# The first batch's spectrum goes straight to its transform rows in SBUF, and the second batch's first sums read their first product from PSUM

## The chip, the cores and the metric

The kernel runs on one core of one Trainium2 chip. The metric is the time of one execution on the device in microseconds (us). The kernel before has a median of 1088.05 us over three runs (1087.7 to 1088.87).

## The reference

There are 8 batches of 4224 positions with 192 channels, in 8 heads of 24. First comes a causal convolution whose 7 taps differ at every position and head and are normalized by a softmax. Its result `x` gets the real part of its two-dimensional Fourier transform added; rows are then normalized and go through an MLP of 192, 768 and 192 channels with a residual.

```python
w = np.exp(weight_gen - np.max(weight_gen, axis=-1, keepdims=True))
w = w / (np.sum(w, axis=-1, keepdims=True) + 1e-09)
out = np.einsum('bshk,bskhg->bshg', w, x_unf)      # x_unf: 7 earlier rows of each position
...
X = np.fft.fft(np.fft.fft(x, axis=1), axis=2)
u = x + np.real(X)
un = (u - mu) / np.sqrt(var + 1e-06)
ch = np.maximum(un @ w_ch1, 0.0) @ w_ch2
return u + ch
```

All tensors are f32; the MLP weights arrive as f64 words, which the kernel turns into f32 itself.

## The kernel before, in words

**Layout.** The 4224 positions are 128 partitions of 33 rows. A batch is worked on in 9 chunks: chunk 8 is row 0, and each of the chunks 0 to 7 is four rows, two from the front (2c+1, 2c+2) and the two mirrored ones from the back, since the transform of a real signal wants both together.

**Convolution, `conv(b)`.** For each chunk and each tap, a product of the shifted rows in `x_sb` and the tap `wp`, spread over 24 channels, is made by VectorE (L762). `x_sb` lies in SBUF, `wp` in PSUM. How the seven products are added depends on the batch. In batch 0 the chunks of `PE_SUMS` (0, 1, 3, 5 and 7) are summed by TensorE, with f32 matmuls by the identity into two PSUM banks `pa` (L767, 128x384 each), which ScalarE copies to `u` (L779). The others are summed by POOL (L771, `u<-u,pr`). A few products of batch 0 are made by ScalarE in pieces of 24 channels (`ACT_TAPS`, L723) or by POOL (`POOL_TAPS`, L760). In batch 1 the chunks 0 and 1 have all their products on POOL; in the chunks 2 to 7 VectorE makes the seven products, the first into `u` itself, does the first of the six adds (`DVE_ADDS`, also L771), and POOL does the other five. From batch 2 on a wide form works on two chunks at once (L847 products on VectorE, L851 adds on POOL).

**Fold and spectrum.** POOL folds a chunk's mirrored rows into `sm` (L794, L795). TensorE multiplies `sm` by a cosine and sine table into `pg` (L803, PSUM tag "fft"). ScalarE keeps a half in `up`, and VectorE forms `gt` from both (L810, L813). Two DMAs for each pair of chunks write `gt` to a DRAM tensor `g_d` (L816, L817).

**Transform, mix and normalization.** `transform(b)` loads `g_d` in blocks of four triples of frequencies with 102 rows (L889, L891), multiplies them by tables (`pp`, L899, tag "fft") and ScalarE copies the result into `pq`. Each of the nine groups of four rows is then mixed: a matmul by the tables (`eo`, L930, tag "fft"), an evacuation on ScalarE to `ot`, and four adds on VectorE into `u` (L936 to L939). Means and variances come from VectorE for the first three groups (L960, L961, `QUICK`), which are also transposed on TensorE with matmuls by the identity (`tr`, L986); the others use ScalarE's sums and a transposing DMA. The steps L974 make the bias of each normalized row, and ScalarE writes `un` (L976).

**MLP.** First layer `ph` (L1060, L1027), rectified to `hh` (L1079, L1080), second layer `po` (L1094), residual on VectorE (L1099), and one output DMA for each half group. The weights' words are turned into f32 by seven VectorE instructions for each piece of 384 columns (L472 to L483) and split into f16 pairs (L488, L489); this is done while batch 0 waits for its transform.

**Filler.** `WARM` puts matmuls of the identity by itself (L538) into TensorE's queue: 14 at the start (`warm_x`) and 40 after the last chunk of batch 0 (`warm`).

**What sets the order.** All instructions are recorded first; `plan()` then lays out each engine's queue with a list scheduler that goes by `cost`, a table of estimated durations. Engines run their queues in order, so an instruction whose data are late holds up everything behind it on that engine. PSUM has eight banks, handed out by tags: "fft" two, "ph" three, "po" two and "wp" one. A tile of a tag can be written only when the tile that had its bank before has been read.

## Time and profile before

| | before |
|---|---|
| median of 3 runs | 1088.05 us |
| span of the profiled execution | 1087.9 us |
| TensorE busy | 1065.5 us (98%) |
| VectorE busy | 958.7 us (88%) |
| POOL busy | 857.1 us (79%) |
| ScalarE busy | 800.0 us (74%) |
| first MLP matmul starts | 100.68 us |

The profile is one execution, whose span is 0.15 us under the median of the runs. PE is TensorE, DVE VectorE, ACT ScalarE, POOL GpSimd and SP SyncE, whose queue issues the DMAs. A row of the groups gives line, engine, operation, output and inputs by the program's names, the shape, the count, busy time and mean ns of one, and behind the second bar the engine's idle time ahead of them with what ended it. Rows of a timeline or of the chain of waits begin with start and length in us. `L` numbers are lines of the kernel before; in the order rows below those of "now" are lines of the changed kernel.

### The profile page before, as it was taken

How to read it: one execution, taken by the hardware profiler on the slowest of the kernel's cores; microseconds unless marked ns; L12 is line 12 of the kernel's file. 1: busy time of each engine (PE TensorE's matmuls, PEld its weight loads, DVE VectorE, ACT ScalarE, POOL GpSimd, SP SyncE). 2: the span in 40 equal slices, each digit the busy share in tenths (PEclk: the TensorE clock that was granted, in tenths of full speed). 3: DMA queues.
4: the chain of work that ended last, by engine and by line, in shares of the span. 5: the costliest groups of instructions: out<-in, count | busy, mean ns of one | idle time of the engine just before them, and what ended most of it. 6: DMA issues, size and time to landing. Idle time of an engine off the chain costs nothing.

```text
span 1087.9 us, 23453 instructions
## 1 busy us (share of the span) xinstructions
PE 1065.5 (98%) x8600; PEld 802.9 (74%) x8600; DVE 958.7 (88%) x1639; ACT 800.0 (74%) x2414; POOL 857.1 (79%) x615
## 2 busy tenths in 40 slices
PE   7899999999999999999999999999999999999998
PEld 5477777787767877777778876887778777786767
DVE  8999999899989999899999999899999998355543
ACT  4666864679966878788786877678786878588842
POOL 5989699899969999799969999699969999011200
PEclk9999999999999999999999999999999999999999
DMA  9353135714492348623582348624582333623311
GB/s 323 129 146 115 34 94 141 202 46 111 119 259 80 85 115 206 170 67 85 129 248 79 92 109 220 157 57 121 122 205 68 83 68 89 140 56 76 79 53 48
DMA packets 171091, 131.20 MB, mean 121 GB/s; under 512 B 119067, under 2 KB 151776, under 8 KB 170976
## 3 DMA queue, kind: packets, MB, share of 16 engines
q1 hardware_dynamic: 170976, 129.70, 45.2%
q8 instruction: 68, 1.11, 0.4%
q14 instruction: 47, 0.39, 0.1%
HBM read 61.46 MB, written 39.37 MB: 93 GB/s over the span
## 4 chain that ended last, share of the span: by engine, by line
PE 66%; DVE 14%; POOL 5%; DMA 4%; ACT 3%; issue 3%; SPq 0%; DVEq 0%; ACTq 0%; POOLq 0%
PE po L1094 27%; PE ph L1060 24%; PE pp L899 5%; PE eo L930 4%; PE ph L1027 3%; DVE pr L847 3%; POOL u L771 2%; PE pg L803 2%; DVE hh L1080 2%; ACT pr L723 1%; DMA ht<-hl 1%; DVE pr L762 1%; POOL u L851 1%; DMA g<-g_d 1%; DMA ring<-ht 1%
## 5 line engine op out<-in xcount | busy, mean ns | idle before, releaser
L851 POOL TENSOR_TENSOR u<-u,pr 128x1536 f32<-128x1536 f32 x144 | 497.0, 3452 | 5.5 <-DVE pr L847 1.7
L1094 PE MATMUL po<-w2h,hh 128*128 128x192 f16 x2832 | 409.2, 247 | 0.0
L1094 PEld LDWEIGHTS <-hh 128*128 128x128 f16 x4248 | 359.1, 98 | 60.1 <-issue 15.2
L1060 PE MATMUL ph<-ht,w1h 128*128 128x512 f16 (+1 forms) x1296 | 382.7, 362 | 0.3 <-ACT ht L987 0.3
L1094 PE MATMUL po<-w2l,hh 128*128 128x192 f16 x1416 | 348.8, 246 | 0.0
L1080 DVE SCALAR_TENSOR_TENSOR hh<-ph,hh 128x512 f16<-128x512 f32 (+1 forms) x390 | 240.5, 636 | 60.9 <-ACT hh L1079 60.5
L1079 ACT ACTIVATE hh<-ph 128x512 f16<-128x512 f32 (+1 forms) x390 | 206.0, 550 | 89.2 <-PE ph L1060 41.0
L847 DVE TENSOR_TENSOR pr<-x_sb,wp 128x1536 f32<-128x1536 f32 x144 | 249.7, 1747 | 7.3 <-POOL u L851 7.3
L1060 PEld LDWEIGHTS <-w1h 128*128 128x128 f16 x1296 | 125.3, 98 | 97.9 <-issue 9.4
L1060 PE MATMUL ph<-ht,w1l 128*128 128x512 f16 (+1 forms) x528 | 181.7, 350 | 0.0
L996 ACT ACTIVATE un<-u,rs 128x192 f32<-128x192 f32 x252 | 122.2, 539 | 40.2 <-POOL rs L994 34.5
L1001 POOL TENSOR_TENSOR hl<-un,hl 128x512 f16<-128x512 f32 (+1 forms) x69 | 74.9, 1086 | 84.3 <-issue 42.5
L771 POOL TENSOR_TENSOR u<-u,pr 128x768 f32<-128x768 f32 (+1 forms) x72 | 117.9, 1649 | 12.2 <-DVE pr L762 11.4
L967 ACT ACTIVATE junk<-u,st 128x192 f16<-128x192 f32 x252 | 114.3, 453 | 4.4
L965 ACT ACTIVATE junk<-u 128x192 f16<-128x192 f32 x252 | 90.8, 360 | 27.6 <-DVE u L939 21.8
L1099 DVE SCALAR_TENSOR_TENSOR u<-po,isc,u 128x384 f32<-128x384 f32 (+1 forms) x122 | 73.1, 599 | 21.1 <-PE po L1094 20.7
L930 PEld LDWEIGHTS eo<-cs_sb,pq 97*128 97x128 f32 x544 | 78.3, 191 | 13.4 <-issue 4.4
L930 PE MATMUL eo<-cs_sb,pq 97*128 97x97 f32 x544 | 85.7, 275 | 0.0
L762 DVE TENSOR_TENSOR pr<-x_sb,wp 128x768 f32<-128x768 f32 (+1 forms) x91 | 74.7, 868 | 2.1 <-POOL u L771 0.7
L1060 PEld LDWEIGHTS <-w1l 128*128 128x128 f16 x528 | 51.9, 98 | 21.6 <-issue 0.5
L794 POOL TENSOR_TENSOR sm<-u 128x382 f32<-128x382 f32 x64 | 64.6, 1009 | 3.7 <-ACT u L779 3.2
L994 POOL TENSOR_TENSOR rs<-st,rs 128x4 f32<-128x4 f32 (+1 forms) x69 | 13.6, 201 | 67.4 <-DVE rs L970 67.3
(130 smaller groups left out, 1538.4 us busy)
## 6 DMA issues: line engine op xcount, KB each, us to landing
out_dram<-u SPq DMA_DIRECT2D x64, 384.0 KB
x_sb<-in_x_dram SPq DMA_DIRECT2D x48, 384.0 KB
g<-g_d SPq DMA_DIRECT2D x40, 336.0 KB
x_sb<-in_x_dram SPq DMA_DIRECT2D x8, 864.0 KB
g_d<-gt SPq DMA_DIRECT2D x32, 195.0 KB
g_d<-gt SPq DMA_DIRECT2D x32, 189.0 KB
w<-in_weight_gen_dram SPq DMA_DIRECT2D x6, 924.0 KB
x_sb<-in_x_dram SPq DMA_DIRECT2D x8, 672.0 KB
```

The lines of the kernel that those rows point to most:

```text
L762: last_product[b] = nc.vector.tensor_tensor(out=dst, in0=rows, in1=wk, op=ALU.mult)
L771: adder.tensor_tensor(out=u, in0=u, in1=pr, op=ALU.add)
L847: last_product[b] = nc.vector.tensor_tensor(out=pr.rearrange("p (s r) (h g) -> p s (r h) g", s=2, g=G), in0=rows, in1=wp[:, :, :, k:k + 1] ...
L851: nc.gpsimd.tensor_tensor(out=u, in0=u, in1=pr, op=ALU.add)
L930: last_mix[b] = nc.tensor.matmul(eo[:, e, j, :], lhsT=pq[0:DH, e, r, r:r + P], rhs=cs_sb[:, e, :], start=True, stop=True)
L965: nc.scalar.activation(junk, uv[t], AF.Identity, scale=-1.0 / D, accum_out=st[:, t, 0:1])
L967: nc.scalar.activation(junk, uv[t], AF.Square, bias=st[:, t, 0:1], accum_out=st[:, t, 1:2])
L996: nc.scalar.activation(un[:, t, :], uv[t], AF.Identity, bias=rs[:, 1, t:t + 1], scale=rs[:, 0, t:t + 1])
L1060: last_ph[n] = nc.tensor.matmul(ph[:, 0:T], lhsT=wt[:, cs_], rhs=ht[:, 0:T, blk], start=(i == 0 and not opens), stop=(i == len(terms) - 1 ...
L1079: nc.scalar.activation(a[:, 0:T], ph[:, 0:T], AF.Relu)
L1080: nc.vector.scalar_tensor_tensor(out=l[:, 0:T], in0=ph[:, 0:T], scalar=0.0, in1=a[:, 0:T], op0=ALU.max, op1=ALU.subtract)
L1094: nc.tensor.matmul(po[t // 2][:, t % 2, :], lhsT=hx[:, t], rhs=wx[:, c2, :], start=(c2 == 0 and i == 0), stop=(c2 == NH - 1 and i == len(t ...
```

## The change

1. **Batch 0's spectrum.** The table of the first transform is sorted so that frequencies 1 to 63 come as 21 triples (`NM`) and 0 and 64 as a block of their own. In batch 0, `gt` goes by DMA from SBUF to `g0`, a view of the space that batch 1's `u` will use later, in 17 large pieces and 18 small ones. Nothing of it is written to DRAM, and `transform(0)` reads `g0` without a load. Later batches still go through DRAM, with one write of 126 rows and one of 2 for each pair of chunks; the zeroing of `g_d` is gone.
2. **First products of batch 0.** In the chunks that TensorE sums, VectorE writes the first product straight into the two banks `pa`; ahead of it three f16 matmuls of the identity open each bank (`open_bank`).
3. **First sums of batch 1 (`ADD_PSUM`).** In the chunks 2 to 7 the first product goes into two PSUM banks `pf` of the tag "fft", 384 columns each, and VectorE's first add reads it there, also in two halves. Folds and spectra of a chunk are put into the next chunk.
4. **Opening.** The groups of chunks are (5,), (6, 7) at the end instead of (5, 6), (7,); chunk 7's product on ScalarE goes back to VectorE; the folds of chunks 5 and 7 run on VectorE. 18 warm matmuls follow chunk 6 in place of 40 after chunk 7. The first three groups are transposed by TensorE's transpose in place of a matmul by the identity.
5. **The planner's costs.** An add on VectorE with both inputs in SBUF is put at 2.0 ns a column instead of 1.042, POOL's products at 1.78, a transpose at one pass, and a DMA from SBUF to SBUF has an issue cost that grows with its rows. This moves instructions throughout the program.

Other edits have no instruction of their own behind them: constants for options that are off (`ONE_BIAS`, `SEEDED`, `PE_WORDS`, `POOL_OWN`, `POOL_WORDS`), `u` in fixed halves by a batch's parity instead of a rotation, and the planner's handling of partition strides. There is one scale more for the MLP (`fsc`).

The diff's core:

```diff
-ACT_TAPS = {(0, 1): (0,), (0, 3): (0,), (0, 5): (0,1), (0, 7): (0,)}
+ACT_TAPS = {(0, 1): (0,), (0, 3): (0,), (0, 5): (0,1)}
-WARM = {-1: 14, 7: 40}
+WARM = {-1: 14, 6: 18}
+DVE_FOLDS = (5, 7)
+OPENING = [(8, 0), (1, 2), (3, 4), (5,), (6, 7)]
...
+    def open_bank(bank):
+        for i in range(0, 2 * D, P):
+            nc.tensor.matmul(bank[:, i:i + P], lhsT=ident16, rhs=ident16, start=(i == 0), stop=False)
...
+                    seeds = pa if i == 0 and mine else None
+                    if ADD_PSUM and i == 0 and DVE_ADDS.get((b, c)):
+                        seeds = firsts[c] = [pst("fft", 2, [P, 512], F32, f"pf_{b}_{c}_{h}") for h in range(2)]
+                    elif seeds:
+                        for bank in seeds:
+                            open_bank(bank)
...
+                        if seeds:
+                            for h in range(2):
+                                last_product[b] = nc.vector.tensor_tensor(
+                                    out=seeds[h][:, 0:2 * D].rearrange("p (n g) -> p n g", g=G), in0=rows[:, h], in1=wk[:, h], op=ALU.mult)
...
+                        if i == 1 and c in firsts:
+                            for h, bank in enumerate(firsts.pop(c)):
+                                nc.vector.tensor_tensor(out=u[:, h], in0=bank[:, 0:2 * D].rearrange("p (r d) -> p r d", r=2), in1=pr[:, h], op=ALU.add)
+                            continue
...
+        if b == 0:
+            for j in range(J):
+                last_g2[0] = nc.sync.dma_start(g0[t2 + j:t2 + j + 6 * NT:NT, 0:NM], gt[0:6 * NM, at + j])
+            for kk in range(2):
+                last_g2[0] = nc.sync.dma_start(g0[kk * NT + t2:kk * NT + t2 + J, NM], gt[6 * NM + kk:6 * NM + kk + 1, at:at + J])
+        elif at == 2 or c == NC:
...
-            nc.sync.dma_start(g_d[0:NK1, 0, ts, :], gt[0:NK1, 0:at + J])
-            nc.sync.dma_start(g_d[1:NK1 - 1, 1, ts, :], gt[NK1:P, 0:at + J])
+            nc.sync.dma_start(g_d[0:NM, :, ts, :].rearrange("m k t d -> k m t d"), gt[0:6 * NM, 0:at + J])
+            nc.sync.dma_start(g_d[NM, 0:2, ts, :], gt[6 * NM:P, 0:at + J])
...
+            if b == 0:
+                g2 = g0[:, m0:m0 + nm]
...
-                    nc.tensor.matmul(tr[i][0:m, t, :], lhsT=un[:, t, i * P:i * P + m], rhs=ident32, start=True, stop=True)
+                    nc.tensor.transpose(tr[i][0:m, t, :], un[:, t, i * P:i * P + m], ident32)
...
+        t = 150 + (6.27 if ins.opcode == "Reciprocal" else 2.0 if slow else 1.042) * n + (60 if len(reads) == 3 and n < 512 else 0)
```

**What moves, first place.** VectorE's queue around the mix of group 0 of batch 0. The names `raw_w`, `pa_w`, `t_w`, `pw_w` and `w2f` are the turning of weight words into f32, `eo` and `ot` are the mix, `u` the rows. Before:

```order
L483 TENSOR_TENSOR w2f<-pw_w_0_1005,t_w_0_1006 128x384
L476 SCALAR_TENSOR_TENSOR pw_w_1_1015<-pa_w_1_1014,t_w_1_1016 128x384
L478 TENSOR_SCALAR pa_w_1_1014<-pw_w_1_1015 128x384
L481 SCALAR_TENSOR_TENSOR t_w_1_1016<-raw_w_416,pa_w_1_1014 128x384
L483 TENSOR_TENSOR w2f<-pw_w_1_1015,t_w_1_1016 128x384
L936 TENSOR_TENSOR eo_0_928<-eo_0_928,ot_0_933 128x2x97
L937 TENSOR_TENSOR eo_0_928<-eo_0_928,ot_0_933 128x194
L938 TENSOR_TENSOR u_0_145<-u_0_145,eo_0_928 128x2x2x97
```

Now, from the last weight steps ahead of the mix on:

```order
L495 TENSOR_SCALAR pa_w_0_977<-raw_w_433 128x384
L517 SCALAR_TENSOR_TENSOR w1l_90<-pw_w_00_878,sc_w_852,w1h_89 128x384
L497 SCALAR_TENSOR_TENSOR t_w_0_979<-raw_w_433,pa_w_0_977 128x384
L1001 TENSOR_TENSOR eo_0_901<-eo_0_901,ot_0_906 128x2x97
L517 SCALAR_TENSOR_TENSOR w1l_90<-pw_w_01_890,sc_w_852,w1h_89 128x384
L1002 TENSOR_TENSOR eo_0_901<-eo_0_901,ot_0_906 128x194
L498 TENSOR_SCALAR pa_w_0_977<-raw_w_433 128x384
L1003 TENSOR_TENSOR u_72<-u_72,eo_0_901 128x2x2x97
L1004 TENSOR_TENSOR u_72<-u_72,eo_0_901 128x2x2x95
L499 SCALAR_TENSOR_TENSOR pw_w_0_978<-pa_w_0_977,t_w_0_979 128x384
```

The first add of `eo_0` stood behind all weight steps and now stands ahead of twelve steps of the second layer's words. Seven of the twelve come before the steps that make group 0's bias (L1043 now), and five behind them.

**Second place.** VectorE's queue in a chunk of batch 1's convolution: `pr` is a product, `pf` a PSUM bank with half the first product. Before, chunk 3:

```order
L762 TENSOR_TENSOR u_2_1368<-x_sb,wp_815 128x768
L762 TENSOR_TENSOR pr_3_1_1464<-x_sb,wp_815 128x768 x2
L771 TENSOR_TENSOR u_2_1368<-u_2_1368,pr_3_1_1464 128x768
L936 TENSOR_TENSOR eo_5_1358<-eo_5_1358,ot_5_1400 128x2x97
L762 TENSOR_TENSOR pr_3_3_1506<-x_sb,wp_815 128x768
```

Now, the same chunk:

```order
L813 TENSOR_TENSOR pf_3_0_1422<-x_sb,wp_789 128x384
L813 TENSOR_TENSOR pf_3_1_1423<-x_sb,wp_789 128x384
L825 TENSOR_TENSOR pr_3_1_1433<-x_sb,wp_789 128x768 x2
L835 TENSOR_TENSOR u_73<-pf_3_0_1422,pr_3_1_1433 128x384
L835 TENSOR_TENSOR u_73<-pf_3_1_1423,pr_3_1_1433 128x384
```

The product of 768 into `u` became two of 384 into PSUM, and the add of 768 two of 384. The two `pr` products stand between them, as before.

**Third place.** SyncE's queue at the end of batch 0's spectrum, now: the pieces of the last two pairs of chunks (`gt_4`, `gt_6`) into `g0`, which is named after the space that it borrows (`u_73`). Before, four writes to DRAM and seven loads stood here.

```order
L876 DMA u_73<-gt_4_474 6x21x192 x4
L878 DMA u_73<-gt_4_474 2x1x192
L876 DMA u_73<-gt_6_659 6x21x192 x4
L878 DMA u_73<-gt_4_474 2x1x192 x3
L878 DMA u_73<-gt_6_659 2x1x192 x4
```

The last pair's rows leave in four large and four small pieces, with three small ones of the pair before among them.

More of the change, by code (lines that the diff above doesn't have):

```diff
@@ L199, in plan @@
                 needs.setdefault(index[first.name], False)
-        price = cost(ins, lane, reads, writes)
+        price = cost(ins, lane, reads, writes, sbuf)
         if joined:
@@ L652, in conv @@
                 keep_warm(pst("fft", 2, [P, P], F32, "warm_x"), WARM[-1])
-        groups = [(NC, 0), (1, 2), (3, 4), (5, 6), (7,)] if b == 0 else [(c,) for c in range(NC + 1)]
+        groups = OPENING if b == 0 else [(c,) for c in range(NC + 1)]
         if b >= WIDE_FROM:
@@ L726, in conv @@
                 for c, R, u, wp, pa, wq, pt, at in chunks:
-                    order = turns(pt, TURNS[len(pt)]) if pt and pa else range(K)
+                    order = turns(pt, TURNS[len(pt)]) if pa and 0 < len(pt) < K else range(K)
                     order = [k for k in order if k not in at] + list(at)
+                    mine = [k for k in range(K) if k not in pt and k not in at]
+                    if pa and mine:
+                        order.sort(key=lambda k: k != mine[0])
                     k = order[i]
```

245 lines of the change are left out of this document (144 added, 101 removed).

## The prediction

> **What bounds the kernel now.** I began with the page: span, busy shares and the chain that ended last.
>
> ```profile
> span 1087.9 us, 23453 instructions
> PE 1065.5 (98%) x8600; PEld 802.9 (74%) x8600; DVE 958.7 (88%) x1639; ACT 800.0 (74%) x2414; POOL 857.1 (79%) x615
> PE 66%; DVE 14%; POOL 5%; DMA 4%; ACT 3%; issue 3%; SPq 0%; DVEq 0%; ACTq 0%; POOLq 0%
> ```
>
> TensorE is busy for 1065.5 of 1087.9 us, so a gain must come from work that TensorE no longer has, from its 22.4 us of idle time, or from "busy" time that is only filler: the warm matmuls. The change touches batches 0 and 1, so I cut the span where the MLP begins and where the second batch is behind, with the view of busy time by window (span, then busy time of PE, PEld, DVE, ACT and POOL with counts, granted clock, DMA share, GB/s).
>
> ```profile
> 60.00:80.00 20.00, 19.75 (x125) 16.08 (x124) 18.43 (x44) 11.08 (x41) 16.16 (x15) 1.00 0.50 150
> 100.40:203.70 103.30, 98.52 (x553) 74.89 (x553) 100.51 (x175) 71.97 (x188) 91.99 (x75) 1.00 0.35 97
> 120.00:200.00 80.00, 75.50 (x425) 59.76 (x424) 78.48 (x133) 52.84 (x146) 75.84 (x62) 1.00 0.41 117
> 203.70:1088.00 884.30, 877.50 (x7603) 665.48 (x7601) 765.06 (x1274) 670.77 (x2001) 681.79 (x469) 1.00 0.45 115
> ```
>
> From 203.70 TensorE idles 6.8 us in 884.3. That stretch is its own; the change leaves its matmuls alone, so I carry its length over. Between 100.40 and 203.70, where batch 1 is convolved while batch 0 runs its MLP, TensorE idles 4.78 us and VectorE only 2.79. Before 100.40 nothing of the MLP has begun, and a microsecond won there moves everything behind it. Two numbers are therefore wanted: when the first MLP matmul starts, and how long the next hundred microseconds take. The chain of waits says what sets each.
>
> ```profile
> 61.15 5.34 ACT pr L723 x26
> 67.67 0.76 DVE wp L580
> 71.91 0.48 DVE pa_w L472
> ...
> 91.55 0.56 DVE w2f L483
> 92.42 0.38 DVE eo L937
> ...
> 96.58 0.56 ACT un L976
> 97.18 2.85 PE tr L986 x14
> 100.04 0.59 ACT ht L987
> 100.68 1.24 PE ph L1060 x5
> ```
>
> From 71.91 to 92.11 the chain holds VectorE work alone: words of the MLP weights turned into floats. The spectrum's way through DRAM, beside it, is not in the chain.
>
> ```profile
> by line: POOL u L771 23.0%; issue 13.0%; DVE pr L762 10.8%; PE ph L1060 10.2%; PE po L1094 6.0%; PE tr L986 3.8%; DVE u L762 2.7%; POOL hl L1001 2.7%; POOL hl L1003 2.3%; PE pp L899 2.3%; DVE wp L573 1.8%; DVE w L574 1.8%; POOL sm L794 1.7%
> ```
>
> This is the same chain grouped by line from 100 to 215 us: the convolution's adds on POOL and its products on VectorE, in turn.
>
> **Term 1, the opening.** The DMA hop first. Rows of SyncE's queue and of TensorE:
>
> ```profile
> 71.45 0.30 SPq L816 DMA_DIRECT2D g_d<-gt  x1
> 75.43 10.54 SPq L889 DMA_DIRECT2D g<-g_d  x6
> 72.31 7.41 PE L538 MATMUL warm<-ident 128*128 128x128 f32 x64
> 79.56 0.87 PE L899 MATMUL pp<-te_sb,g 102*97 102x102 f32 x8
> 89.95 2.21 PE L930 MATMUL eo<-cs_sb,pq 97*128 97x97 f32 x16
> ```
>
> From the last write's issue (71.45) to the first transform matmul (79.56) pass 8.1 us: 4.0 for the write up to the load's issue, 4.1 for the load. One direct hop takes the place of two. But it is issued in pieces, in the new order four large DMAs and seven small ones in a row (the last pair's, and three of the pair before); at 0.30 us of queue each the last leaves 3.3 us late and the saving is 4.1 − 3.3 = 0.8. If the first transform block needs only part of them it is nearly 4. So the first transform matmul moves by −4 to 0 us, and later than before only if one scatter lands slower than write plus load. The eo product ends its first eight matmuls at about 91.1 (89.95 plus half of 2.21), and VectorE takes it up at 92.0, when its weights are done. Unless VectorE gets there earlier, the saved hop turns into waiting; so VectorE's count decides.
>
> ```profile
> L762 DVE TENSOR_TENSOR pr<-x_sb,wp 128x768 f32<-128x768 f32 x79 | 71.3, 946 | 2.1 <-POOL u L771 0.7 <-PE pa L767 0.7 <-DMA x_sb<-in_x_dram 0.5
> L472 DVE TENSOR_SCALAR pa_w<-raw_w 128x384 int32<-128x384 int32 x6 | 3.3, 553 | 0.1
> L938 DVE TENSOR_TENSOR u<-u,eo 128x388 f32<-128x388 f32 x64 | 35.5, 554 | 0.6
> ```
>
> Added on VectorE ahead of group 0: the product of chunk 7 that ScalarE gives back, +0.95; five first products written as two 384-wide halves into PSUM, 5 × (2 × 0.553 − 0.946) = +0.8; two folds, each one add of 382 (0.55 by the last row) and one of two columns, an estimated 0.05, together +1.2. That is +2.95. Moved: twelve weight steps of 0.55 us, 6.6 us in all, now stand behind the first add of eo_0. So that add comes 3.7 us earlier, as far as the hop allows. But the first normalized row (`un`) is released by four small steps on VectorE (L974 before), and seven of the twelve stand ahead of those again. By then only five have been passed over, −2.75, and with them eo_1's first three adds, which stood ahead of the four before and stand behind them now: −1.27 (from 92.02 to 93.29 for the same three of eo_0, rows under rival D). Net at `un`: +2.95 − 2.75 − 1.27 = −1.07 us. Bounds: −3.7, if the seven only fill VectorE's waits for ScalarE, and +0.2, if the three adds stay on the path. I take −1.0.
>
> The transposes come next in the chain, 2.85 us of f32 matmuls by the identity. As true transposes they may take one pass where a f32 matmul takes two. No transpose is in this trace. Bounds: 0, and half of 2.85, −1.4; I take −1.0, since the rows must still be loaded. Term 1 is −2.0 us: first MLP matmul at 98.7 instead of 100.68. Edits with one answer: ten `pa` matmuls fewer lie under waits for VectorE's products; thirty f16 identity matmuls open banks ahead of data; the 22 warm matmuls fewer are filler.
>
> **Term 2, batch 1's convolution.** Groups between 99.8 and 203.7, by shape:
>
> ```profile
> L771 DVE TENSOR_TENSOR u<-u,pr 128x768 f32<-128x768 f32 x6 | 10.1, 1675 | 0.1
> L762 DVE TENSOR_TENSOR u<-x_sb,wp 128x768 f32<-128x768 f32 x6 | 5.7, 952 | 0.1
> L771 POOL TENSOR_TENSOR u<-u,pr 128x768 f32<-128x768 f32 x35 | 64.9, 1867 | 8.5 <-DVE pr L762 8.4
> ```
>
> Removed on VectorE: 5.7 + 10.1 = 15.8 us. Added: 12 products of 384 into PSUM and 12 adds of 384 from PSUM and SBUF, 24 × 0.55 = 13.2 by L472 and L938; with the small overlap that successive rows show (starts 0.47 apart), 12.8. So VectorE has 3.0 us less here. What it is worth: at most TensorE's idle time, 4.78; nothing, if POOL, whose five adds per chunk stay, sets the pace (75.84 busy of 80). POOL itself may win: the spread of its adds, and of VectorE's six, shows each slowing the other.
>
> ```profile
> L771 POOL TENSOR_TENSOR u<-u,pr x72: 587/1817/2540, 10.9 to 199.0; 128x768 f32<-128x768 f32 x60, 128x192 f32<-128x192 f32 x12
> L771 DVE TENSOR_TENSOR u<-u,pr x6: 958/1698/2411, 122.0 to 175.6; 128x768 f32<-128x768 f32 x6
> ```
>
> VectorE's add takes 0.96 us at best and 2.41 at worst. With its first operand in PSUM that collision goes; POOL's 30 adds after 120 would drop from 1.868 towards the 1.817 median, −1.5 us, or by a collision's 0.7 (2.54 − 1.82) at six places, −4.3. The Trainium skill, page "SBUF — State Buffer", section "SBUF: two separate sides", says that a VectorE operation with two SBUF inputs and a GpSimd operation that reads SBUF lock each other out for a whole instruction. The two rows agree with that. I take −3.0 for term 2.
>
> **Term 3, the rest.** Two more table loads on ScalarE:
>
> ```profile
> L575 ACT ACT_TABLE_LOAD x8 | 10.3, 1283 | 0.9 <-PEq L1231 0.7
> ```
>
> Two of 1.28 us lie on an engine busy 671 of 884 us; I take 0, bound +2.6. The writes of later batches, 126 + 2 rows for 65 + 63, keep their bytes: 0. Later first groups read unchanged rows.
>
> Sum: 1087.9 − 2.0 − 3.0 = 1082.9 us for the profiled execution. Its span lies 0.15 below the median of the runs (1088.05), so 1083.1 in rounded figures.
>
> **The rivals.**
>
> *B, more is won.* Both engines come free of each other (−4.78, all of TensorE's idle time) and the opening keeps its lead of −3.7: 1087.9 − 8.5 + 0.15 = 1079.6. For it: the chain is POOL and VectorE in turn. Against it: new waits on the shared banks.
>
> *C, nothing is won.* POOL keeps its pace, 75.84 of 80 us, and what the opening wins becomes waiting for it: 1088.0. This is also what the change not doing its work looks like. For it: POOL's count of adds is unchanged. Against it: POOL idles 8.4 us for VectorE's products before its block, so it can start sooner.
>
> *D, slower: the two "fft" banks.* The pair `pf` takes both banks that the spectrum, the transform and the mix share, from the first product until the add: two products 1.1, two `pr` products 1.9, two adds 1.1, about 4.1 us for each of six chunks. An eo product or a spectrum that stands in TensorE's queue behind it stops the MLP matmuls behind that. The mix holds a bank for its four adds, 1.83 us by these rows:
>
> ```profile
> 92.02 0.36 DVE L936 TENSOR_TENSOR eo<-eo,ot 128x194 f32<-128x194 f32 x1
> 92.42 0.37 DVE L937 TENSOR_TENSOR eo<-eo,ot 128x194 f32<-128x194 f32 x1
> 92.82 0.56 DVE L938 TENSOR_TENSOR u<-u,eo 128x388 f32<-128x388 f32 x1
> 93.29 0.54 DVE L939 TENSOR_TENSOR u<-u,eo 128x380 f32<-128x380 f32 x1
> ```
>
> One such wait per chunk costs 6 × 1.83 = 11.0: 1083.1 + 11.0 = 1094.1. It outweighs the gain from 5.0 / 6 = 0.83 us per chunk. Against it: the order was laid out with these banks known, and other work is in the queue.
>
> *E, the clock.* With 18 warm matmuls, 36 passes of 7.41 / 64 = 0.116 us, TensorE is kept busy for 4.2 us instead of 9.3 and may stand idle before the transform. Earlier in the trace it stood 3.87 us, and then:
>
> ```profile
> 10.36 9.70 PE L767 MATMUL pa<-pr,ident 128*128 128x384 f32 x24 [3.87 <-DVE pr L762]
> 11.00:15.00 4.00, 4.00 (x8) 2.09 (x7) 4.00 (x5) 3.55 (x19) 1.90 (x4) 0.57 1.05 406
> ```
>
> The granted clock fell to 0.57 over 4 us, 1.7 us of TensorE work lost: 1083.1 + 1.7 = 1084.8. The Trainium skill, page "TensorE: Matmul & The Clock Gate", section "Part 1: The HAM clock gate", has the clock halved after an idle window of about 3.4 us; the trace agrees with 3.87 idle. Against it: a hop of 4.0 and pieces of 3.3 less 4.2 of warm work leave 3.1 us, less than 3.87.
>
> **How the numbers follow.** Forecast A 0.38 (1083.1; own range 1080.5 to 1085.5), E 0.05, B 0.18, C 0.18, D 0.21. About 0.2% of the time, 2.2 us, is what a measurement of this kernel can tell from no change. A, E and B are faster by more: 0.61. C is the same: 0.18. D is slower: 0.21. The range reaches down past B, where the hop's whole −4 and −1.4 for the transposes would stand in place of −3.7 (1087.9 − 4.78 − 5.4 + 0.15 = 1077.9, set at 1077.0 for the small idle times behind), and up into D, to three quarters of its price (1083.1 + 8.3 = 1091.4, rounded to 1091.5).
>
> **What would show it.** Right: first MLP matmul near 98.7; VectorE's first sums near 0.55 per half instead of 1.675 whole, POOL's adds nearer 1.8; TensorE's idle time from there to the first wide product about 2 us; the rest 884 us long as before. Wrong: TensorE waiting at `eo` or `pg` for VectorE's `pf` adds (D); POOL full with VectorE waiting for its adds (C); a granted clock of about 0.5 at the transform (E); or a longer rest, which no term here foresees.

## The result, and the profile after

The changed kernel takes 1103.83 us in the median of four runs (1098.70 to 1109.58), the kernel before 1088.46 us (1087.70 to 1091.69): a ratio of 1.0139, with a 95% interval of 1.0101 to 1.0177. It is 15 us slower; the forecast was 1083.1.

The page of the changed kernel: span and busy shares.

```profile
span 1103.8 us, 23375 instructions
PE 1066.6 (97%) x8542; PEld 803.1 (73%) x8542; DVE 956.4 (87%) x1661; ACT 793.3 (72%) x2400; POOL 850.3 (77%) x610
```

TensorE is as busy as before (1065.5 us), although 22 warm matmuls and ten of `pa` are gone, and it idles 37.2 us instead of 22.4. Both need an explanation. I cut the span at two events that both kernels have: the first MLP matmul, and VectorE's first wide product (the 1536-wide one into `u`, the first of the third batch). Windows of before, then of after:

```profile
0.00:100.68 100.68, 89.50 (x447) 62.57 (x447) 93.16 (x192) 57.50 (x227) 83.59 (x73) 0.98 0.59 193
100.68:199.41 98.73, 94.38 (x528) 70.80 (x527) 96.20 (x170) 68.83 (x181) 90.24 (x72) 1.00 0.34 95
199.41:1087.90 888.49, 881.64 (x7627) 669.56 (x7626) 769.34 (x1278) 673.63 (x2008) 683.26 (x472) 1.00 0.45 115
```

```profile
0.00:100.75 100.75, 81.90 (x405) 57.88 (x406) 89.75 (x186) 53.40 (x198) 75.65 (x64) 0.94 0.53 174
100.75:208.60 107.85, 101.05 (x538) 75.86 (x538) 96.61 (x202) 72.19 (x188) 92.24 (x78) 0.94 0.31 93
208.60:1103.80 895.20, 883.69 (x7602) 669.35 (x7600) 770.06 (x1275) 667.67 (x2016) 682.36 (x469) 1.00 0.45 114
```

The opening keeps its length (+0.1 us), the second stage grows by 9.1, the long third stage by 6.7. In the second stage the granted clock, the third number from the end of a row, was 0.94 for 1.00, and TensorE idles 2.5 us more (6.80 for 4.35). In the third stage it idles 11.51 us for 6.85. The places of the slow clock, by windows:

```profile
75.78:82.61 6.83, 6.06 (x36) 6.09 (x37) 2.24 (x7) 3.04 (x12) 5.96 (x4) 0.50 0.54 182
99.68:106.50 6.82, 5.35 (x16) 2.35 (x17) 6.76 (x26) 3.91 (x8) 6.82 (x5) 0.50 0.00 0
150.88:157.70 6.82, 6.46 (x21) 5.24 (x22) 5.46 (x12) 3.38 (x8) 5.81 (x6) 0.50 0.54 172
580.96:587.78 6.82, 5.69 (x34) 5.59 (x35) 3.16 (x4) 1.91 (x8) 6.74 (x4) 0.50 0.96 215
```

Each loses up to 3.4 us (0.50 × 6.8), 13.6 in all; 6.3 of it lie in the second stage (0.50 × 5.75 behind 100.75, and 3.4). Before had one stretch of 3.4 us at 11 to 15, 1.7 us lost, and the changed kernel has that one as well (10.93 to 14.34). Each of the four follows a stall. TensorE's timeline ahead of them:

```profile
71.08 1.61 PE L567 MATMUL warm<-ident 128*128 128x128 f32 x12
76.55 1.65 PE L964 MATMUL pp<-te_sb,u 102*97 102x102 f32 x8 [3.86 <-DMA u<-gt]
...
97.96 1.32 PE L1055 MATMUL tr<-ident,un 128*128 128x128 f32 x6 [1.85 <-ACT un L1045]
99.62 0.67 PE L1055 MATMUL tr<-ident,un 128*128 128x128 f32 x2 [0.34 <-ACT un L1045]
100.75 0.58 PE L1129 MATMUL ph<-ht,w1h 128*128 128x512 f16 x1 [0.46 <-ACT ht L1056]
102.63 0.58 PE L1129 MATMUL ph<-ht,w1h 128*128 128x512 f16 x1 [0.87 <-DVE t_w L504]
...
151.24 1.65 PE L863 MATMUL pg<-sm,f_sb 128*128 128x192 f32 x4 [3.43 <-POOL sm L855]
```

The first stall is for the direct hop. The second is a row of small ones, the last for weight words (`t_w`) that hold the banks of `ph`. The third is a spectrum standing in TensorE's queue ahead of MLP matmuls, while POOL still folds. The fourth is in the chain of waits:

```profile
568.62 8.03 DMA ht<-hl
...
576.72 0.67 SPq L1081
...
577.50 4.55 DMA g<-g_d
...
582.09 3.04 PE pp L964 x16
```

SyncE's queue holds the copy behind a transposing DMA (L1081), and the loads of the fifth transform stand behind it. The transposition took 8.0 us to land.

The hop's cost in SyncE's queue, first by line and then in the timeline:

```profile
L878 SPq DMA_DIRECT2D u<-gt x18: 557/598/725, 33.6 to 76.0; - x18
L876 SPq DMA_DIRECT2D u<-gt x17: 725/771/1205, 32.7 to 71.4; - x17
```

```profile
68.53 3.64 SPq L876 DMA_DIRECT2D u<-gt  x4
72.21 4.31 SPq L878 DMA_DIRECT2D u<-gt  x7
```

A piece holds the queue for 0.60 or 0.77 us, and the last eleven for 7.95 us. VectorE meanwhile, and ScalarE, which it waits for:

```profile
80.90 0.62 DVE L517 SCALAR_TENSOR_TENSOR w1l<-pw_w,sc_w,w1h 128x384 f16<-128x384 f32 x1 [4.52 <-ACT w1h L516]
...
90.52 0.36 DVE L1001 TENSOR_TENSOR eo<-eo,ot 128x194 f32<-128x194 f32 x1
```

```profile
78.23 0.35 ACT L968 COPY pq<-pp 97x204 f32<-97x204 f32 x1 [6.67 <-PE pp L964]
...
80.27 0.60 ACT L516 ACTIVATE w1h<-pw_w,sc_w 128x384 f16<-128x384 f32 x1
```

The scaling of the first weight piece stands in ScalarE's queue behind copies of the transform, which wait for the hop; so VectorE's chain of weight words, which nothing else held, stood 4.52 us. Last, the groups of the second batch's convolution, 100 to 205 us:

```profile
L813 DVE TENSOR_TENSOR pf<-x_sb,wp 128x384 f32<-128x384 f32 x12 | 6.4, 558 | 0.2
L835 DVE TENSOR_TENSOR u<-pf,pr 128x384 f32<-128x384 f32 x12 | 6.2, 550 | 0.1
```

```profile
L838 POOL TENSOR_TENSOR u<-u,pr 128x768 f32<-128x768 f32 x36 | 65.0, 1810 | 7.2 <-DVE u L835 5.6 <-DVE pr L825 1.2
```

The new operations cost what was forecast (0.55 us), and POOL's adds fell from 1867 to 1810 ns. VectorE still idles 11.2 us in the second stage (107.85 − 96.61), where it idled 2.5; the largest wait is this row of the view of waits, for a small matmul on the way to the second layer's scale:

```profile
DVE m_w L475 <- PE mr_w L474: 4.8, 1, 4.8
```

One more change lies in the third stage, in the transforms of the later batches. The view of windows for the tile `pp` alone (busy time of PE, PEld and ACT), before, and in e8, a run below that has the changed tables and no slow clock in this stage:

```profile
199.41:1087.90 888.49, 63.53 (x616) 59.97 (x616) 49.50 (x196) 1.00 0.45 115
204.45:1099.50 895.05, 65.62 (x616) 60.82 (x616) 50.05 (x210) 1.00 0.45 114
```

The 616 matmul records take 2 us longer in e8 and 4 us longer in the changed kernel (67.8), part of which is its slow clock at 581. In the four other traces made from the kernel before that have no slow clock in this stage (e1, e2, e14, e17) they take 62.3 to 63.5 us, in e4, e5, e10, e12 and e13, with the changed tables, 65.0 to 66.8. The records that differ are those of the last block, now frequencies 0 and 64: their contraction runs over 34 rows where it was 68, and their mean grew from 236 to 272 ns. Why fewer rows take longer is not shown here.

### The profile page after: what moved, and what is told of

Read it like the earlier page. It is cut to its first block, busy times and chain, and to the rows that moved or that the text cites. A ratio compares the mean times of both kernels' runs of the same rounds, so it can differ in the third digit from the quotient of the medians.

```text
span 1103.8 us, 23375 instructions
## 1 busy us (share of the span) xinstructions
PE 1066.6 (97%) x8542; PEld 803.1 (73%) x8542; DVE 956.4 (87%) x1661; ACT 793.3 (72%) x2400; POOL 850.3 (77%) x610
## 4 chain that ended last, share of the span: by engine, by line
PE 69%; DVE 13%; DMA 6%; POOL 5%; ACT 3%; issue 3%; SPq 1%; DVEq 0%; POOLq 0%; ACTq 0%
PE po L1172 28%; PE ph L1129 24%; PE pp L964 6%; PE eo L995 4%; DMA ht<-hl 4%; PE ph L1096 3%; POOL u L916 3%; PE pg L863 3%; DVE pr L825 3%; DVE pr L912 2%; DVE hh L1149 2%; POOL u L838 1%; DMA ring<-ht 1%; ACT pr L771 1%; DVE u L1180 1%
## 5 line engine op out<-in xcount | busy, mean ns | idle before, releaser
L1148 ACT ACTIVATE hh<-ph 128x512 f16<-128x512 f32 (+1 forms) x390 | 207.4, 551 | 105.0 <-PE ph L1129 48.2
L825 DVE TENSOR_TENSOR pr<-x_sb,wp 128x768 f32<-128x768 f32 (+1 forms) x87 | 71.0, 861 | 0.0
L968 ACT COPY pq<-pp 97x204 f32<-97x204 f32 (+1 forms) x96 | 31.6, 329 | 51.7 <-PE pp L964 49.1
```

Source lines behind the costliest of these rows:

```text
L825: last_product[b] = nc.vector.tensor_tensor(out=dst, in0=rows, in1=wk, op=ALU.mult)
L1148: nc.scalar.activation(a[:, 0:T], ph[:, 0:T], AF.Relu)
```

## The experiments

Theory: TensorE's stalls, and the slow clock behind them, make the loss, and single parts of the change make the stalls. Rival: the order of the queues makes them. Ratios are to the kernel before on the same chip, with their 95% interval. "Stages" are the three lengths as above (before 100.7, 98.7, 888.5; changed kernel 100.7, 107.9, 895.2), of the profiled execution. A median moves by up to 3 us with the slow stretches that an execution happens to have: the kernel before itself had medians of 1087.6 to 1090.5 in the various sets of runs. Of the runs made from the changed kernel only e6 and e7 have an interval that does not overlap the changed kernel's own (1.0101 to 1.0177); what the others say rests on their traces. The planner lays the program out again for every edit, so each run also has an order of its own.

**e1: fewer warm matmuls before.**

```diff
-WARM = {-1: 14, 7: 40}
+WARM = {-1: 14, 7: 14}
```

> The kernel before with 14 warm matmuls in place of 40 after batch 0's last chunk; nothing else is edited. By the profile of before, TensorE would then stand idle for about 5.9 us ahead of its first transform matmul (warm work ends near 73.7, the matmul starts at 79.56). Clock theory (most of the 15.9 us is the slow clock after such stalls: four stretches of 6.8 us at half clock, 3.4 us lost in each): granted clock 0.5 around 77 to 84, the transform's matmuls 1.6 us a group of eight in place of 0.9, the first MLP matmul 1.5 to 3.4 us later than 100.68, the whole 1.5 to 3.4 us longer: 1089.6 to 1091.5. Rival (the slow clock only accompanies waits that new queue orders make; the warm matmuls are filler): 1088.0, within 0.5.

Ratio 1.0018 (1.0000 to 1.0035), stages 102.0, 101.5, 885.8.

```profile
80.11 1.65 PE L899 MATMUL pp<-te_sb,g 102*97 102x102 f32 x8 [5.20 <-issue]
```

```profile
77.00:85.00 8.00, 4.89 (x32) 4.92 (x32) 7.24 (x16) 2.61 (x10) 8.00 (x6) 0.57 0.58 148
```

The clock fell as the clock theory says, and the groups of eight took 1.6 us. Little of the 3.4 us lost reached the first MLP matmul, which came 1.3 us later (102.00): VectorE began its words 1.0 us later to start with (L472 at 72.81 for 71.83), as this order has it, and they set the mix as before. The warm matmuls hold the clock up; that the whole gains by them, about 2 us, is not clear of noise (the interval begins at 1.0000).

**e2: transposes alone, in the order of before.**

```diff
-nc.tensor.matmul(tr[i][0:m, t, :], lhsT=un[:, t, i * P:i * P + m], rhs=ident32, start=True, stop=True)
+nc.tensor.transpose(tr[i][0:m, t, :], un[:, t, i * P:i * P + m], ident32)
```

> The kernel before with TensorE's transpose in place of matmuls by the identity for the first three groups; the queues' orders stay as they were. If a transpose takes half the time: the 2.85 us of the first group's transposes become 1.4 to 1.9, the first MLP matmul starts 1.0 to 1.4 earlier than 100.68, the whole 1086.6 to 1087.1. Clock theory with the addition that transposes do not count as work for the clock: the granted clock falls to 0.5 near 100 for some 7 us, as it does in the changed kernel at 99 to 107, and the whole is 1089 to 1091. Rival (a transpose counts as any matmul): no clock below 1 there.

Ratio 0.9976 (0.9963 to 0.9989): the only kernel here that is faster than before. Median 1087.02 beside 1090.46. Stages 100.5, 98.3, 886.1.

Group 0's transposes before, and then in e2:

```profile
97.18 3.19 PE L986 MATMUL tr<-ident,un 128*128 128x128 f32 x16 [0.28 <-ACT un L976]
97.89 1.75 PE L986 MATMUL tr<-ident,un 128*128 128x128 f32 x8 [0.28 <-ACT un L976]
100.52 0.38 PE L1060 MATMUL ph<-ht,w1h 128*128 128x512 f16 x1 [0.88 <-ACT ht L987]
```

```profile
97.00:104.00 7.00, 5.54 (x32) 2.83 (x31) 6.83 (x30) 5.53 (x12) 7.00 (x6) 1.00 0.47 163
```

The transposes of the first group take 1.75 us where the matmuls took 3.19; 0.6 of the saving goes into a longer wait for ScalarE's copy (0.88 for 0.31). The clock stays at 1.00. Were transposes no work to it, TensorE would have stood for 2.9 us here (0.28, 1.75 and 0.88), and stalls of 2.0 us had a slow clock behind them in e5; so they count. In this execution the mix began about 0.7 us later than in before's, so that the first MLP matmul came only 0.2 earlier. The rest of the gain lies behind it, in the second and third group: from the first MLP matmul to the end TensorE is busy for 973.1 us where it was 976.0, and the span is 3.0 us shorter (1084.9).

**e3: 40 warm matmuls in the changed kernel** (`6: 18` becomes `6: 40`).

> The changed kernel with 40 warm matmuls in place of 18 after chunk 6. They fill the 3.86 us in which TensorE stands ahead of its first transform matmul at 76.55. Clock theory: no slow clock there, the transform ends 3.4 us earlier (88.5 to about 85.1), the whole up to 3.4 us shorter: 1100.4 where the changed kernel has 1103.8, less if VectorE's weight words then set the mix. Rival (order alone): 1103.8, within the changed kernel's own spread of 1098.7 to 1109.6.

Ratio 1.0095 (1.0064 to 1.0126), median 1100.35; stages 98.4, 104.2, 894.0. TensorE's timeline, then VectorE's:

```profile
75.84 0.91 PE L964 MATMUL pp<-te_sb,u 102*97 102x102 f32 x8 [0.48 <-issue]
...
98.40 0.59 PE L1129 MATMUL ph<-ht,w1h 128*128 128x512 f16 x1 [0.56 <-ACT ht L1056]
```

```profile
78.80 0.62 DVE L517 SCALAR_TENSOR_TENSOR w1l<-pw_w,sc_w,w1h 128x384 f16<-128x384 f32 x1 [1.02 <-ACT w1h L516]
...
88.68 0.37 DVE L1001 TENSOR_TENSOR eo<-eo,ot 128x194 f32<-128x194 f32 x1
```

The median is 3.5 us shorter, as forecast, though within the changed kernel's spread, as the rival had it; the trace decides. There is no slow clock at the transform, VectorE waits 1.02 us for L516 and not 4.52, takes up the mix at 88.68, and the first MLP matmul comes at 98.4: the opening is worth 2.3 us once TensorE does not stand. The later stages keep most of their loss; a slow stretch stays at 98 to 105, and another came at 135 to 139, behind a stall of 2.1 us.

**e4: matmuls by the identity in place of the changed kernel's transposes** (the edit of e2 backwards).

> The changed kernel with matmuls by the identity in place of the transposes for the first three groups. If transposes do not count as work for the clock, the slow stretch from 99 to 107 goes and 3.4 us with it, less about 1.0 for the longer matmuls: 1101.4 for 1103.8. If they count, the slow stretch stays and the whole is about 1.0 longer. Rival (order alone): as the changed kernel, within its spread.

Ratio 1.0082 (1.0054 to 1.0110), median 1099.90; stages 99.4, 101.2, 896.4.

```profile
97.00:104.00 7.00, 6.61 (x22) 3.74 (x21) 6.89 (x27) 3.33 (x7) 7.00 (x5) 0.51 0.00 0
```

The slow stretch near 100 stays, so the transposes do not cause it, as e2 said. The median is 4 us shorter where 1.0 longer was expected, which is still within the changed kernel's spread: in this order the stall ahead of the transform was 1.43 us and no slow clock followed.

**e5: the second batch's sums as before** (`ADD_PSUM = 0`).

> The changed kernel with the second batch's first sums as before (first product into SBUF, first add of 768 with both inputs in SBUF, folds at a chunk's own end). Theory of the banks (the pair of fft banks and the later folds make TensorE stand at a spectrum, 3.43 us at 148 to 151, and slow the clock behind it, 3.4 more): 1097 for 1103.8, no wait over 2 us at a spectrum matmul between 120 and 200, the first ten residuals of the MLP no later than 2 us behind before (5.7 in the changed kernel). Rival (the gain on VectorE is real and the loss lies elsewhere): the sums cost 3.0 us again, 1104 to 1107.

Ratio 1.0108 (1.0086 to 1.0130), median 1100.77; stages 99.1, 103.6, 893.6. 3 us better, half of what the theory of the banks asked, and it loses 4.9 us in the second stage without any `pf`. A spectrum still stood in the queue, for 2.28 us at 187 (waiting for VectorE's `gt`), with a slow clock behind it, which that theory had excluded. The sums are not the main cause.

**e6: the planner's old costs in the changed kernel** (the whole function `cost` as before).

> The changed kernel with the planner's table of costs as before, all else as changed. Theory of the order (the new costs lay the queues out so that waits come late in the program as well; from the 28th to the last of the MLP's residuals the changed kernel loses 8.6 us on before): that loss falls under 3 us, the whole to about 1097. Clock theory (stalls and slow clock come from the hop and the banks): 1101 to 1106, and the loss behind the 28th residual stays above 5.

Ratio 1.459 (1.457 to 1.462), median 1589.07. The run tells little of the two theories: the old table also prices DMAs within SBUF otherwise, and the order falls apart; TensorE waits 210 us for loads of `g` in nine waits. It shows how far an order alone can move this program, and no more.

**e7: the second weight piece in the banks `po`** (`if i < 2` becomes `if i < 1` in `prep_w2`).

> The changed kernel with the second piece of the second layer's weight words in the banks po in place of ph. In the changed kernel the second pair of first-layer matmuls waits for these words' last steps at 101.7 to 102.6, and runs with a slow clock to 107. Theory of the words (twelve steps moved behind the mix still hold two of the three ph banks): the first group's MLP runs on from its first matmul, 3 to 6 us earlier by its fifth matmul, no slow clock near 100, the whole 1098 to 1101. Rival (TensorE waits there for the normalized rows and the transposes anyway): within 1 us of 1103.8 less the clock's chance.

Ratio 1.0073 (1.0056 to 1.0090), median 1097.25; stages 100.9, 105.8, 888.7. The whole is a little shorter than the theory's 1098 to 1101, but not in the way it says. The first stage did not gain, and the wait for the words moved from `ph` to the transposes (2.4 us for `t_w`, L504). Of the 8.3 us that the profiled execution gained, 6.5 are in the third stage, which this edit does not touch.

**e8: the first batch through DRAM, 40 warm matmuls** (`if b == 0` in `spectrum` and `transform` never holds).

> The changed kernel with the first batch's spectrum written to DRAM and loaded again as for the later batches, and 40 warm matmuls so that TensorE does not stand. If the direct hop is worth its 3.0 us at the first transform matmul (76.55 for 79.56): that matmul near 79.5, the first MLP matmul 2 to 3 us later, the whole 1102 to 1107. Rival (VectorE's words set the opening, and the hop's gain goes into a stall and a slow clock): first MLP matmul at 100 to 101 as in both kernels, the whole 1098 to 1102 for want of the slow clock at 76 to 83.

Ratio 1.0146 (1.0119 to 1.0174), median 1104.87; stages 100.6, 103.8, 895.0. First transform matmul at 78.85, first MLP matmul at 100.62. Beside the changed kernel (100.75) the hop seems worth nothing, as the rival says, but the whole missed the rival's 1098 to 1102. The run to set it beside is e3, which has the same 40 warm matmuls and the direct hop: there these matmuls came at 75.84 and 98.40. With TensorE kept busy, the direct hop is worth 3.0 us at the transform and 2.2 at the first MLP matmul, as the first theory said; in the changed kernel the stall and the slow clock take it back.

**e9: the first weight piece ahead of the transform's copies on ScalarE** (the weights are recorded before the transform, whose copies are held behind the first L516).

> The changed kernel with the first scaled weight piece on ScalarE (L516) put ahead of the transform's copies in ScalarE's queue. In the changed kernel VectorE stands 4.5 us from 76.4 for it, since it comes behind the copies of the first transform matmuls, which wait for the hop. Theory of the opening (the weight words, late by that wait, are what holds the first groups): that wait goes, VectorE takes up the first mix 2 to 4 us earlier than 90.5, TensorE's first MLP matmul comes near 98 and the twelfth near 104 (100.8 and 108.0 in the changed kernel), the whole 3 to 5 us shorter than 1103.8. Rival (the hop at 76.55 and the slow clock behind it set the mix): mix at 90, the whole within 1.5 of the changed kernel.

Ratio 1.0138 (1.0092 to 1.0184), median 1102.53; stages 101.2, 101.0, 898.5. L516 came at 74.8 for 80.3, but VectorE's wait only moved to the next piece (4.1 us), and the mix began at 91.3. The stall at the hop (3.38 us) and the slow clock behind it stayed, and so did the opening: the rival held, that these set the mix. The second stage is 7 us shorter; the third gave back 3.

**e10: the small pieces through DRAM.** Five writes and one load for 18 pieces:

```diff
-            for kk in range(2):
-                last_g2[0] = nc.sync.dma_start(g0[kk * NT + t2:kk * NT + t2 + J, NM], gt[6 * NM + kk:6 * NM + kk + 1, at:at + J])
+            if at == 2 or c == NC:
+                nc.sync.dma_start(g_d[NM, 0:2, t2 - at:t2 + J, :], gt[6 * NM:P, 0:at + J])
```

> The changed kernel with the 18 small pieces of the hop (two frequencies, 1.5 KB each) replaced by five writes to DRAM and one load, which only the last block of the transform needs; the 17 large pieces stay. By the changed kernel's rows the seven small ones behind the last large piece hold SyncE's queue for 4.3 us. Theory of the pieces: the first transform matmul comes 2 us earlier than 76.55, TensorE stands under 2 us and no slow clock follows at 76 to 83; transform done 4 us earlier; the whole 2 to 4 us shorter. Rival (one hop's landing sets it): first transform matmul at 76 to 77.

Ratio 1.0106 (1.0071 to 1.0142), median 1099.90; stages 98.2, 105.0, 893.4. The whole gained as expected, but only half by the mechanism: the first transform matmul came at 76.04, as the rival said, behind a stall of 2.1 us, with a slow clock at 77 to 80, and the first MLP matmul stood at 98.2. But the clock was slow behind it for 10 us:

```profile
97.00:108.00 11.00, 7.95 (x25) 2.96 (x24) 10.90 (x38) 5.66 (x14) 11.00 (x8) 0.53 0.00 0
```

**e11: e9 and e10 together; e12: the same with `ADD_PSUM = 0`.**

> The edits of the two runs before together in the changed kernel. If the opening's loss is these two: first MLP matmul at 96 to 98, no slow clock between 74 and 100, the whole 1096 to 1099, the rest of the loss in the second batch's convolution. Rival: no better than the better of the two by more than 1 us.

> As the run before, with the second batch's first sums as in the kernel before. If the two fft banks and the later folds cost more than the 3.0 us that VectorE is spared: 2 us or more shorter than the run before, 1092 to 1096, with no wait over 2 us at a spectrum matmul. If the sums are a gain: 2 to 3 us longer than the run before.

e11: ratio 1.0131 (1.0093 to 1.0168), median 1101.18; stages 101.3, 101.0, 895.0. e12: 1.0150 (1.0110 to 1.0191), 1103.03; stages 99.8, 103.3, 896.2. In e11 the clock was slow at 79 to 82 and at 99 to 102, which its first expectation excluded. Two mends that seemed good for 4 and 1 us make 3 together, and the sums from PSUM are a gain of 2 in this pair, where e5 had them a loss of 3. None of these differences is clear of the intervals: effects of single parts are no larger than what a new order does by the way.

**e13 and e14: the order from both sides.** e13 is the changed kernel with the old costs of VectorE, POOL and transposes only; e14 the kernel before with the new ones of VectorE and POOL. e14 has the same instructions as before.

```diff
-        t = 150 + (6.27 if ins.opcode == "Reciprocal" else 1.042) * n + (60 if len(reads) == 3 and n < 512 else 0)
+        slow = len(reads) == 2 and n > 64 and all(ap.tensor.name in sbuf and ap.ap[-1][0] for ap in reads)
+        t = 150 + (6.27 if ins.opcode == "Reciprocal" else 2.0 if slow else 1.042) * n + (60 if len(reads) == 3 and n < 512 else 0)
...
-        t = 183 + (1.92 if out.dtype == F16 else 2.13) * n
+        t = 183 + (1.92 if out.dtype == F16 else 1.78 if any(ap.ap[-1][0] == 0 for ap in reads) else 2.13) * n
```

> The changed kernel with the planner's old costs for VectorE, POOL and transposes alone; the costs of DMAs stay new. Theory of the order (these costs lay the queues out worse late in the program): the loss on before from the 28th of the MLP's residuals to the last falls from 8.6 us to under 3, the whole to 1096 or less. Rival (the late loss comes with the changed data paths or by chance of clock and DMA): it stays between 2 and 9, the whole at 1098 to 1105.

> The kernel before with the planner's new costs for VectorE's and POOL's operations; no instruction is added or removed, only the order moves. Theory of the order: 3 to 8 us longer than before, with a part of it behind 350 us. Rival: within 2 us of before.

e14: ratio 1.0052 (1.0034 to 1.0071), median 1095.06 beside 1090.17; stages 100.0, 102.0, 892.5. Order alone costs 5 us. The second stage is 3.2 us longer and the third 4.0, but the cut between them is an event on VectorE, and this order leaves TensorE about 3 us more work behind it. Counted from the first MLP matmul to the end, the length grows by 7.2 us: 4.1 more idle time and 3.1 more busy time, for the same 8154 matmul records, with one slow stretch (186 to 193, 3.4 us lost). TensorE's waits between 60 and 300 show where:

```profile
PE po L1095 <- DVE m_w L451: 3.5, 1, 3.5
PE po L1095 <- DVE gt L814: 2.6, 1, 2.6
```

e13: ratio 1.0128 (1.0092 to 1.0163), median 1102.25; stages 98.3, 105.4, 895.0. Going back to the old engine costs does not mend the changed kernel; here the theory of these costs failed and its rival's numbers held. The costs of DMAs stayed new in it and were not tried alone.

**e15: the sums from PSUM alone, in the kernel before** (the `pf` lines of the diff, with folds and spectra at a chunk's own end).

> The kernel before with the second batch's first product in two fft banks and VectorE's first sum from there, nothing else. My forecast's term: 3.0 us shorter, 1085.0. Theory of the banks: TensorE waits at spectra and mixes for them, 2 us or more longer, with waits at a spectrum or eo matmul between 120 and 200 that before does not have.

Ratio 1.0320 (1.0297 to 1.0342), median 1124.14; stages 101.2, 134.0, 888.0. VectorE's queue shows why:

```profile
140.71 0.54 DVE L759 TENSOR_TENSOR pf<-x_sb,wp 128x384 f32<-128x384 f32 x1
142.82 0.36 DVE L823 TENSOR_TENSOR gt<-pg,up 128x194 f32<-128x194 f32 x1 [1.57 <-ACT up L822]
...
143.48 0.56 DVE L759 TENSOR_TENSOR pf<-x_sb,wp 128x384 f32<-128x384 f32 x1
```

The second half-product of a chunk needs the fft bank that the spectrum of the chunk before holds, and that waits for POOL's five adds and the fold: the chunks come one after the other. TensorE runs out of work; its longest waits are 10.5 us for `m_w` and 10.3 for a load of `g`.

**e16: the old opening in the changed kernel** (`OPENING`, `ACT_TAPS`, `DVE_FOLDS` and `WARM` as before).

> The changed kernel with the first batch's chunks grouped as before ((5, 6), (7,)), chunk 7's product on ScalarE again, all folds on POOL and 40 warm matmuls after chunk 7. Theory of the opening (the new grouping ends the spectrum 2.5 us earlier, and the hop's stall eats that): first transform matmul 1 to 3 us later, first MLP matmul within 1.5 us of 100.7, the whole within 3 us of the changed kernel. Rival (folds on VectorE and the early end of the spectrum cause the stalls): 5 us or more shorter.

Ratio 1.0145 (1.0115 to 1.0174), median 1105.79; stages 99.8, 106.5, 900.0. Within 3 us of the changed kernel, with the first transform matmul 2.0 us later (78.55), as the theory of the opening said.

**e17: e15 with the later folds of the changed kernel.**

```diff
+                if b == 1 and i == 1 and grp[0] > 1:
+                    while tails:
+                        finish(*tails.pop(0)[:5])
...
-            while tails and not (b == 1 and grp[0] == 0):
+            while tails and not (b == 1 and grp[0] < NC):
```

> The kernel before with the second batch's first sums read from PSUM and, as in the changed kernel, a chunk's fold and spectrum recorded behind the next chunk's first sum. My forecast's term: 3.0 us shorter than before, 1085 to 1087. Theory of the banks: the pair of fft banks still makes mixes, spectra and products wait for each other, 3 us or more longer than before, 1091 or more. Theory of the serial chunks alone: the 34 us of the run without late folds go, and the result is within 2 us of before.

Ratio 1.0015 (0.9994 to 1.0035): the same as before. The profiled execution has 1085.2 us, stages 100.3, 95.8, 889.1, and no slow clock but that of the first 15 us. The second stage, and POOL's adds in it:

```profile
100.28:196.12 95.84, 93.08 (x526) 70.15 (x526) 90.44 (x179) 67.95 (x179) 89.54 (x76) 1.00 0.33 98
```

```profile
L798 POOL TENSOR_TENSOR u<-u,pr 128x768 f32<-128x768 f32 x36 | 65.5, 1830 | 6.2 <-DVE u L795 5.8
```

In this execution the second stage is 2.9 us shorter than before, with TensorE's idle time down from 4.35 to 2.76. The 34 us of e15 were the serial chunks. In the median nothing of the 2.9 is left: the interval leaves room for a gain of 0.6 us at most. The profiled execution is the second fastest of its set and has a mean clock of 0.998, as has the fastest; in seven others it is 0.993 to 0.997 (one execution, of 2196.78 us, is left out). Whether the part itself lowers the clock there is not shown.

**e18: three mends together** (e3, e7 and e10).

> The changed kernel with 40 warm matmuls, the second weight piece in the banks po, and the small pieces of the hop through DRAM, which alone brought it to 1100.4, 1097.3 and 1099.9 from 1103.8. If they add up: 1103.8 - 3.5 - 6.6 - 3.9 = 1090. If they are one loss that shows in different places (a stall ahead of the MLP, with or without a slow clock): 1096 to 1099.

Ratio 1.0199 (1.0160 to 1.0238), median 1111.44: slower than any of them, and in the median than the changed kernel; stages 99.9, 107.7, 902.7. Both expectations missed. The planner laid out yet another order, in which TensorE waits 8.0 us for loads of `g` behind 300 us, six times.

## Why the prediction was wrong

**Term 1, the opening: forecast −2.0, measured +0.1.** The first transform matmul did come 3.0 us earlier (76.55), within the −4 to 0 given. The step that failed is the price of the pieces, 0.30 us of queue each, and with it the bound on the stall that rests on it. 0.30 is what a write from SBUF to DRAM took. The trace of before has copies within SBUF too, and they hold the queue for twice as long (ns, least, median and most):

```profile
L1012 SPq DMA_DIRECT2D ring<-ht x56: 600/618/1056, 248.9 to 1042.3; - x56
```

The pieces took 0.60 and 0.77, the last eleven 7.95 us and not 3.3. The change itself had the figure: its new cost of such a DMA is 600 ns and 1.5 for each of its rows, 0.60 and 0.79 us. So TensorE stood 3.86 us and not under 3.1, the clock halved, the first transform matmuls took 1.65 us for 0.87, ScalarE's copies of them came late, L516 stood behind these copies, and VectorE, whose count the prediction followed, waited 4.52 us for L516. The count was not the error: in e3, with the stall filled, the mix began 3.3 us earlier than before (the prediction has 3.7), and the first MLP matmul came at 98.40 (98.7). e9, which took L516 out from behind the copies and kept the stall, gained nothing there. The other traces with the direct hop agree: with a stall of up to 2.35 us ahead of the transform the first MLP matmul came at 98.2 to 99.9 (e3, e4, e5, e10, e12, e13, e16, e18), with 3.3 to 3.9 at 100.75 to 101.3 (e7, e9, e11, the changed kernel).

Two smaller errors lie in this term. The five weight steps "passed over" have no price: they hold banks of `ph`, and TensorE stood for them 2 us after its first MLP matmul; e7 moved the words to other banks, and the wait went to the transposes. And of the three groups that are transposed only the first is priced; e2 shows 2.9 us of TensorE work less behind it.

**Term 2, the sums from PSUM: forecast −3.0.** The mechanism is seen where the part stands alone with its later folds: VectorE's new operations cost 0.55 us, POOL's adds are shorter, and in e17's profile the stage is 2.9 us shorter. The median of e17 does not have that gain, so the size is not shown. In the changed kernel the stage is 9.1 longer; of that up to 6.3 us is the clock (e17 has none of it) and 2.5 idle time. The fear in rival D, a spectrum standing ahead of MLP matmuls, came true once, for 3.43 us; as the sole cause it is ruled out, since e5, without `pf`, loses 4.9 us in the stage.

**Rival E, the clock, at 0.05 and 1.7 us.** This was the worst estimate. The stall at the hop was 3.86 us, not under 3.1; the clock was slow for two spans of 3.4 us and not for one, 3.4 us lost; and it happened four times, 13.6 us in all. My rule that only a wait as long as 3.87 us counts had one row behind it. e3 had a slow stretch behind 2.1 us.

**Term 3, the rest "carried over": forecast 0, measured +6.7.** The step that failed is the sentence that the change leaves the third stage alone since its matmuls stay. Its order does not stay: the planner lays out the whole program again, and e14, with the same instructions and other costs, shows that this alone costs 5 us. Nor do all matmuls stay as they were: with the new last block the later transforms take 2 to 4 us more of TensorE. Since the stages are cut at an event on VectorE, the two behind the first MLP matmul are better taken together, before, e14 and the changed kernel:

```profile
100.68:1087.90 987.22, 976.02 (x8154) 740.36 (x8153) 865.55 (x1448) 742.46 (x2188) 773.50 (x543) 1.00 0.44 113
99.98:1094.40 994.42, 979.12 (x8154) 741.14 (x8153) 866.54 (x1447) 742.88 (x2188) 779.01 (x546) 1.00 0.44 112
100.75:1103.80 1003.05, 984.74 (x8138) 745.21 (x8137) 866.67 (x1477) 739.86 (x2203) 774.60 (x547) 0.99 0.43 111
```

The changed kernel is 15.8 us longer here: 7.1 us of idle time and 8.7 of busy time. In the busy time the slow clock has up to 9.7 us (0.50 × 19.4), the last blocks 2 to 4, and the transposes take 2.9 off. So the loss is accounted for, but not all of it is traced to a part: e7 shortened this length by 8.5 us with an edit at 100 us, and e13 took the engine costs back and kept 13.2 of the 15.8. Which instructions the new order puts in whose way, behind 200 us above all, stays open. In the traces made from the kernel before with its costs and without serial chunks this length is 984.4 to 987.3 us (e1, e2, e17), in those made from the changed kernel 994.6 to 1010.3, leaving out e6.

So the two theories are not rivals in the end: the loss is mostly stalls and slow clock, as the first said, but only the stall at the hop is traced to one part; others come with the order, as the second said, and no single part that was undone took more than half of the loss away. The hop, the new last block and the opening were not run alone in the order of before, as the transposes (e2) and the sums (e17) were.

## What to carry to other kernels

When a planner decides the order, a change of its costs is a change of the whole program: compare orders on the engines that wait, and ask of each moved instruction which in-order neighbour it now stands behind, before adding up busy times. TensorE at 98% is a warning: at the hop a stall of 2 to 4 us cost 1.7 to 3.4 more at the slow clock, so an edit that shortens work but opens a gap can lose on both. Price a new instruction from a row of its own kind: a copy within SBUF from another such copy, not from a write to DRAM. Try the parts of a large change alone in the old order; here the transposes alone were faster than both kernels.

## What was not expected of the hardware

The slow clock comes in spans of 3.41 us at half speed, mostly one or two of them, 1.7 or 3.4 us lost in a stretch; e10 has three in a row (97 to 108) and e15 five (192 to 209). One long standing was not needed. Ahead of the first transform matmul, a stall of 0.48 to 1.71 us had no slow clock behind it (e3, e18, e4, e16, e13), one of 2.00 to 2.35 us had one span (e5, e10, e12), one of 3.33 to 3.86 us one or two (e11; e7, e9, the changed kernel), and one of 5.20 us two (e1). After 99 us in the changed kernel waits of 1.85, 0.34 and 0.46 us within 5 us came ahead of it. The Trainium skill, page "TensorE: Matmul & The Clock Gate", section "Part 1: The HAM clock gate", has a window of 3413 ns that is free-running, so that the point of a change depends on where in the window a matmul lands. The trace agrees: the slow stretches of the changed kernel begin 18, 25, 40 and 166 times 3.413 us behind the end of its first one (75.78, 99.68, 150.88 and 580.96, behind 14.34). A DMA from SBUF to SBUF with 126 rows held SyncE's queue for 0.77 us, and one of two rows for 0.60, where one from SBUF to DRAM took 0.31 to 0.33 in the median (`g_d<-gt`, before).
